# A chunked RWKV7 kernel: the state turned by VectorE transposes, state and score products joined into one of 128 rows, 40 columns for w

## The chip, the cores and the metric

The kernel runs on one core of a Trainium2 chip. The metric is the device time of one execution in microseconds (us). Most executions of one kernel lie within a per cent or so; a run more than 1.5% above the fastest of its kernel is called slow and is left out of the ratios. TensorE does the matmuls, VectorE (DVE in the profile) the elementwise work, ScalarE (ACT) copies and activations, GpSimd (POOL) three multiplications per unit, and the sync queue (SP) issues most transfers. The **granted clock** is the TensorE clock that the profile shows, as a share of full speed. An **eviction** is the copy of a matmul's result out of its PSUM bank, where the matmuls write, by VectorE or ScalarE.

## The reference

For each of 4 batches and 8 heads, a 40x40 state runs through 768 tokens. A feed-forward block with SiLU follows. All of it is float32.

```python
def _attn_ref(r, k, v, w, a, b):              # each (4, 8, 768, 40)
    state = np.zeros((B, H, D, D))
    for t in range(S):
        y[:, :, t] = einsum('bhd,bhde->bhe', r_t, state)
        Sa = einsum('bhde,bhe->bhd', state, a_t)
        state = state * w_t[:, :, None, :] - einsum('bhd,bhe->bhde', Sa, b_t)
        state = state + einsum('bhd,bhe->bhde', v_t, k_t)

def _moe_ref(x, w_in, w_out):                 # x: 3072 x 320, d_ff = 2048
    h = x @ w_in
    return ((h / (1.0 + np.exp(-h))) @ w_out).astype(np.float32)
```

## The kernel before

The 768 tokens are cut into 12 chunks of 64. Batches go in two pairs, so a chunk has two **units** and there are 24 units. A unit passes through `keys` (transposes), `right` (right-hand sides), `solve`, `read`, `write` (new state and outputs) and `turn` (the state transposed for the next chunk's `write`). Two chunks ahead, `prepare` scales the inputs (VectorE scan and reciprocal, then GpSimd) and makes the negated scores. Once per two chunks, `invert` inverts the triangular matrices of both: the scores go out to memory and back, then 31 rows are worked off one after another on VectorE, then merged. That falls in the **odd** chunks. The feed-forward block, called **moe** here, is woven in between as soon as two chunks of outputs are there. The order of each engine's instructions is fixed when the kernel is built. The line numbers (L501 and so on) are those of the profile.

```python
# prepare, two chunks ahead
def scale():
    ...                                                                   # VectorE scan, L262
    pin(nc.vector.reciprocal(R, u.W[:, :, 1 : C + 1]))                    # L263, 3.35 us
    nc.gpsimd.tensor_tensor(out=u.a, in0=u.a, in1=u.W[:, :, 0:C], op=ALU.mult)               # L264
    nc.gpsimd.tensor_tensor(out=u.kb[:, :, 1], in0=u.kb[:, :, 1], in1=R, op=ALU.mult)        # L265
    ...                                                                   # the third multiplication, L271
...
def between(u, n, s):      # scores: n=1 negated, for the inverse; n=0 for the scores times v
    pm = [bank("pm") for _ in range(2)]
    ...
    nc.tensor.matmul(pm[j][C * be : C * be + C, p * C : p * C + C],       # L236, four 64x64 tiles
                     lhsT=u.kb[J, q, n, :], rhs=u.a[J, q, :], start=True, stop=True)
    ...                                                                   # masked evictions, L244
...
def row(t):                # the inverse: 31 rows, each needs the one before
    x = nc.vector.tensor_tensor(out=part, in0=X[L, :, t + 1 : N, t + 1 : N], in1=..., op=ALU.mult)     # L327
    x = nc.vector.tensor_reduce(out=X[L, :, t + 1 : N, t], in_=part, axis=AX.X, op=ALU.add)            # L334
...
# the unit's own chain
def right():
    between(u, 0, u.sk)
    pr = [bank("pr") for _ in range(2)]
    for p in range(P if u.n > 0 else 0):
        for be in range(2):
            nc.tensor.matmul(pr[be][C * be : C * be + C, p * 80 : p * 80 + 80],              # L513
                             lhsT=u.a[:, P * be + p, :], rhs=gbd[:, P * be + p], start=p == 0, stop=False, ...)
    for p in range(P):
        for j in range(2):
            for be in range(2):
                mark["right"] = nc.tensor.matmul(pr[be][R, p * 80 + j * D : p * 80 + j * D + D],   # L525
                             lhsT=u.sk[R, j, p, :], rhs=u.v2[R, 2 * p + j, :], ...)
...
def turn():
    pt = [bank("pt") for _ in range(2)]
    for q in range(Q):
        for j in range(2):
            mark["turn"] = nc.tensor.matmul(pt[j][DP * j : DP * j + D, q * DP : q * DP + DP],      # L587
                             lhsT=gbd[J, q, j], rhs=ident[J, J], start=True, stop=True).ins
    for j in range(2):
        nc.scalar.copy(out=gt[R].rearrange("p q e -> p (q e)"), in_=pt[j][R])                     # L596
```

Of the kernel before, what the change touches and what calls it, by code (L numbers as in the profile page):

```python
# [27 lines left out]
DP = 64  # L28
# [13 lines left out]
def kernel(  # L42
# [37 lines left out]
    ms = sb.tile([128, 2, C], F32, name="ms")  # L80
# [3 lines left out]
    nc.vector.tensor_copy(out=ms[:, 0], in_=ml)  # L84
    nc.vector.tensor_scalar(out=ms[:, 1], in0=ml, scalar1=-1.0, scalar2=None, op0=ALU.mult)
# [8 lines left out]
    Gbd = [sb.tile([128, Q, 2, D], F32, name=f"Gbd{m}") for m in range(NM)]  # L94
    GT = [sb.tile([128, Q, DP], F32, name=f"GT{m}") for m in range(NM)]
    RHS = [sb.tile([128, P, 2, DP], F32, name=f"RHS{m}") for m in range(NM)]
# [111 lines left out]
    def load(u, what="abk", queue=nc.sync):  # L208
        B2 = slice(2 * u.m, 2 * u.m + 2)
        if "a" in what:  # L210
            u.a = sb.tile([128, Q, C], F32, name="a", bufs=4)
            send(queue, u.a.rearrange("p (b q) t -> p b (q t)", b=2), aT[B2, u.n].rearrange("b p c -> p b c"))
        if "b" in what:
            u.kb = sb.tile([128, Q, 2, C], F32, name="kb", bufs=6)
        for n, x in ((1, bT), (0, kT)):
            for be in range(2 if "kb"[n] in what else 0):
                send(queue, u.kb[:, P * be : P * be + P, n], x[2 * u.m + be, u.n].rearrange("p (q t) -> p q t", q=P))
# [10 lines left out]
    def between(u, n, s):  # L228

        pm = [bank("pm") for _ in range(2)]  # L230
        for p in range(P):
            for be in range(2):
                for j in range(2):
                    q = P * be + p
                    J = slice(DP * j, DP * j + DP)
                    nc.tensor.matmul(  # L236
                        pm[j][C * be : C * be + C, p * C : p * C + C],
                        lhsT=u.kb[J, q, n, :],
                        rhs=u.a[J, q, :],
                        start=True,  # L240
                        stop=True,
                    )
        for j in range(2):
            x = nc.vector.tensor_tensor(  # L244
                out=s[:, j],
                in0=pm[j][:, 0 : P * C].rearrange("p (q t) -> p q t", q=P),
                in1=ms[:, n].unsqueeze(1).to_broadcast([128, P, C]),
                op=ALU.mult,
            )
            if n == 1 and u.n < 2:  # L250
                in_order(x, "vector")

    sbs, mark = {}, {}

    def pre(u, md):
        def scale():
            u.W = sb.tile([128, Q, C + 1], F32, name="W", bufs=6)
            R = u.w[:, :, 1 : C + 1]
            pin = partial(in_order, line="vector") if u.n < 2 else lambda x: x
            for be in range(2):  # L260
                W, w = (x[:, P * be : P * be + P].rearrange("p q t -> p (q t)") for x in (u.W, u.w))
                pin(nc.vector.tensor_tensor_scan(W, w, one.rearrange("p q t -> p (q t)"), 0.0, ALU.mult, ALU.add))  # L262
            pin(nc.vector.reciprocal(R, u.W[:, :, 1 : C + 1]))  # L263
            nc.gpsimd.tensor_tensor(out=u.a, in0=u.a, in1=u.W[:, :, 0:C], op=ALU.mult)  # L264
            nc.gpsimd.tensor_tensor(out=u.kb[:, :, 1], in0=u.kb[:, :, 1], in1=R, op=ALU.mult)  # L265
            if u.n > 1:
                keys()
# [9 lines left out]
        def scores():  # L277
            if u.m == 0:
                sbs[u.n] = sb.tile([128, NM, 2, P, C], F32, name="sb", bufs=2)
            between(u, 1, sbs[u.n][:, u.m])  # L280
# [180 lines left out]
    def load_v(u):  # L461
        u.v2 = sb.tile([128, H, D], F32, name="v2", bufs=2)
        T = slice(C * u.n, C * u.n + C)
        for be in range(2):
            nc.sync.dma_start(u.v2[C * be : C * be + C].rearrange("p h d -> p (h d)"), v[2 * u.m + be, T, :])

    def load_r(u, wait=None):
        u.r = sb.tile([128, Q, C], F32, name="r", bufs=2)
        u.vut = sb.tile([128, Q, 2, C], F32, name="vut", bufs=2)
# [20 lines left out]
    def chain(u, xs):  # L490
        X = XT[u.n % 2][:, u.m]
        gbd, gt, rhs = Gbd[u.m], GT[u.m], RHS[u.m]
# [13 lines left out]
        def right():  # L506
            u.sk = sb.tile([128, 2, P, C], F32, name="sk", bufs=2)
            between(u, 0, u.sk)
            pr = [bank("pr") for _ in range(2)]

            for p in range(P if u.n > 0 else 0):
                for be in range(2):
                    nc.tensor.matmul(  # L513
                        pr[be][C * be : C * be + C, p * 80 : p * 80 + 80],
                        lhsT=u.a[:, P * be + p, :],
                        rhs=gbd[:, P * be + p],
                        start=p == 0,
                        stop=False,
                        skip_group_check=True,
                    )  # L520
            for p in range(P):
                for j in range(2):
                    for be in range(2):
                        R = slice(C * be, C * be + C)
                        mark["right"] = nc.tensor.matmul(  # L525
                            pr[be][R, p * 80 + j * D : p * 80 + j * D + D],
                            lhsT=u.sk[R, j, p, :],
                            rhs=u.v2[R, 2 * p + j, :],
                            start=u.n == 0 and p == 0 and j == 0,
                            stop=True,  # L530
                            skip_group_check=True,
                        )
            for be in range(2):
                R = slice(C * be, C * be + C)
                x = nc.scalar.copy(
                    out=rhs[R, :, :, 0:D],
                    in_=pr[be][R, 0 : H * D].rearrange("p (q j d) -> p q j d", q=P, j=2),
                )
                if u.n == 0:
                    behind(x, issued["scalar"])  # L540

        def solve():
            pu = [bank("pu") for _ in range(2)]
            pw = [bank("pw") for _ in range(2)]
# [3 lines that stand above are left out]
# [4 lines left out]
                            rhs=rhs[R, p, j, 0:D],  # L552
# [10 lines left out]
            for p in range(P):  # L563
                for j in range(2):
                    for be in range(2):
                        R = slice(C * be, C * be + C)
                        nc.tensor.matmul(
                            pw[be][DP * j : DP * j + DP, p * C : p * C + C],
                            lhsT=rhs[R, p, j, :],
                            rhs=X[R, P * j + p, :],  # L570
                            start=True,
                            stop=True,
                        )
            for be in range(2):
                nc.scalar.activation(
                    out=u.vut[:, P * be : P * be + P, 1, :],
                    in_=pw[be][:, 0 : P * C].rearrange("p (q t) -> p q t", q=P),
                    func=AF.Copy,
                    scale=-1.0,
                )  # L580

        def turn():
            pt = [bank("pt") for _ in range(2)]
            for q in range(Q):
                for j in range(2):
# [3 lines left out]
                        lhsT=gbd[J, q, j],  # L589
# [28 lines left out]
        def write():  # L618
# [25 lines left out]
            for be in range(0 if last else 2):  # L644
                for j in range(2):
                    J = slice(DP * j, DP * j + DP)
                    g = gbd[J, P * be : P * be + P, j]
                    nc.vector.tensor_tensor(out=g, in0=gy[be][J, :, 0:D], in1=g, op=ALU.add)  # L648
            for j in range(0 if last else 2):
                J = slice(DP * j, DP * j + DP)  # L650
                g = gbd[J, :, j]
# [127 lines left out]
    for t in RHS + Gbd + GT + XT:  # L779
# [242 lines left out]
```

## Time and profile before

| | before |
|---|---|
| time, median of 3 runs | 963.82 us (963.7 to 967.04) |
| span of the profiled run | 967.4 us |
| TensorE / VectorE busy | 86% / 58% |
| chunks 4 to 9, pairs of an even and an odd one | 132.5, 129.5, 123.0 us |

The page and the windows are shown in the prediction. One view also belongs here: VectorE's timeline where odd chunk 7 begins (its key transposes start at 560.06 us). Columns of a timeline: start us, duration us, engine, line, operation, output and inputs, shapes, number of instructions in the step, and in brackets the idle time ahead with what ended it.

```profile
558.41 1.28 DVE L262 TENSOR_TENSOR_SCAN W<-w,one 128x260 f32<-128x260 f32 x2
...
559.92 3.34 DVE L263 RECIPROCAL w<-W 128x512 f32<-128x512 f32 x1
...
574.25 3.35 DVE L263 RECIPROCAL w<-W 128x512 f32<-128x512 f32 x1
...
592.27 0.15 DVE L327 TENSOR_TENSOR tmp<-XI,mi 128x1 f32<-128x1 f32 x1
```

The first unit's scan and reciprocal run as the odd chunk opens, the second unit's 14 us later, and the first row of the inverse 32.2 us after the keys. This is a chain: scan, reciprocal, GpSimd, scores, eviction, the scores' way through memory, rows. VectorE's busy share does not show it.

### The profile page before, as it was taken

To read this page: it belongs to the slowest core of one execution; us is meant where nothing else is said; L and a number is where in the kernel's file an instruction comes from. 1 tells how busy PE (TensorE), PEld (TensorE's weight loads), DVE (VectorE), ACT (ScalarE), POOL (GpSimd) and SP (SyncE) were. 2 spreads that over 40 slices of the span, in tenths; PEclk is the share of its full clock that TensorE was granted. 3 is DMA by queue.
4 is the path that set the end of the run, shared out by engine and by line. 5 is a ranking of instruction groups with operands and counts; after the bars stand their busy time and mean duration, and the time that the engine had idled before them with its cause. 6 is when DMAs were issued, how large, how long until landed. Compare 5 with 4: busy or idle time off the path is not lost.

```text
span 967.4 us, 26530 instructions
## 1 busy us (share of the span) xinstructions
PE 833.7 (86%) x11586; PEld 588.1 (61%) x11586; DVE 564.6 (58%) x1141; ACT 290.9 (30%) x661; POOL 97.4 (10%) x98
## 2 busy tenths in 40 slices
PE   2247088979999949999989999899999999999996
PEld 2236077745778814787646876548865577755544
DVE  8777988976216798164894366972649823031120
ACT  3144356531323212332213341224231142210110
POOL 5121021100001110001010020200110000000000
PEclk9999558989759979997999999999999999999999
DMA  6975516542115530445512555223522213002001
GB/s 141 206 182 128 139 49 171 143 107 65 44 41 137 116 94 18 97 106 113 137 38 45 124 120 119 69 55 92 117 58 62 83 35 73 2 8 66 1 0 31
DMA packets 217626, 83.06 MB, mean 86 GB/s; under 512 B 181536, under 2 KB 209440, under 8 KB 217504
## 3 DMA queue, kind: packets, MB, share of 16 engines
q1 hardware_dynamic: 202384, 76.98, 33.7%
q10 hardware_dynamic: 15120, 4.33, 2.3%
q8 instruction: 92, 1.51, 0.6%
q14 instruction: 30, 0.25, 0.1%
HBM read 67.11 MB, written 14.16 MB: 84 GB/s over the span
## 4 chain that ended last, share of the span: by engine, by line
PE 58%; DVE 28%; DMA 6%; issue 3%; ACT 2%; SPq 1%; POOL 0%; ACTq 0%; POOLq 0%; DVEq 0%
PE po L714 16%; PE ph L698 11%; DVE tmp L327 5%; DVE XI L334 4%; PE pl L603 4%; PE ph L703 4%; DVE w L263 3%; PE pm L236 3%; PE pt L501 3%; PE pq L429 2%; PE pu L549 2%; PE pr L525 2%; DVE gts L707 2%; DVE Gbd L648 2%; PE po L446 2%
## 5 line engine op out<-in xcount | busy, mean ns | idle before, releaser
L714 PE MATMUL po<-wo_s,gts 128*128 128x320 f32 x768 | 221.6, 441 | 5.2 <-DVE gts L707 5.2
L698 PE MATMUL ph<-xt,wi_s 128*128 128x512 f32 (+1 forms) x448 | 195.9, 575 | 25.4 <-DVE gts L707 14.9
L714 PEld LDWEIGHTS po<-wo_s,gts 128*128 128x128 f32 x768 | 142.1, 190 | 67.1 <-DVE gts L707 7.2
L698 PEld LDWEIGHTS ph<-xt,wi_s 128*128 128x128 f32 x448 | 83.9, 201 | 110.9 <-issue 58.2
L707 DVE TENSOR_TENSOR gts<-ph,sg 128x512 f32<-128x512 f32 (+1 forms) x112 | 65.6, 607 | 137.7 <-ACT sg L706 137.6
L706 ACT ACTIVATE sg<-ph 128x512 f32<-128x512 f32 (+1 forms) x112 | 54.4, 533 | 234.8 <-PE ph L703 234.6
L327 DVE TENSOR_TENSOR tmp<-XI,mi 64x2 f32<-64x2 f32 (+40 forms) x169 | 80.8, 478 | 14.4 <-DMA mi<-md 10.8
L263 DVE RECIPROCAL w<-W 128x512 f32<-128x512 f32 x24 | 80.3, 3347 | 1.1
L334 DVE TENSOR_REDUCE XI<-tmp 64x2 f32<-64x2 f32 (+40 forms) x169 | 76.2, 451 | 3.9
L236 PE MATMUL pm<-a,kb 64*64 64x64 f32 x1536 | 48.9, 240 | 18.4 <-POOL kb L265 17.4
L703 PE MATMUL ph<-xt,wl_s 64*128 64x512 f32 (+1 forms) x224 | 62.2, 602 | 0.0
L265 POOL TENSOR_TENSOR kb<-kb,w 128x512 f32<-128x512 f32 x24 | 29.3, 1219 | 302.4 <-DVE w L263 232.4
L244 DVE TENSOR_TENSOR sk<-pm,ms 128x256 f32<-128x256 f32 x48 | 18.1, 416 | 68.8 <-PE pm L236 68.7
L236 PEld LDWEIGHTS pm<-a,kb 64*64 64x64 f32 x1536 | 39.5, 148 | 30.2 <-POOL kb L265 19.7
L264 POOL TENSOR_TENSOR a<-a,W 128x512 f32<-128x512 f32 x24 | 28.6, 1190 | 269.1 <-DMA a<-in_aT 175.2
L603 PEld LDWEIGHTS pl<-r,vut 64*128 64x128 f32 x768 | 49.9, 205 | 6.6 <-issue 2.8
L603 PE MATMUL pl<-r,vut 64*128 64x64 f32 x768 | 51.0, 290 | 2.7 <-DVE vl L611 2.6
L611 DVE TENSOR_TENSOR vl<-pl,ml 128x512 f32<-128x512 f32 x48 | 31.2, 684 | 35.9 <-PE pl L603 35.6
L596 ACT COPY GT<-pt 40x512 f32<-40x512 f32 x44 | 25.5, 580 | 80.9 <-PE pt L587 80.4
L525 PE MATMUL pr<-v,sk 64*64 64x40 f32 x768 | 34.5, 234 | 16.8 <-ACT kt L502 15.6
L525 PEld LDWEIGHTS pr<-v,sk 64*64 64x64 f32 x768 | 29.9, 141 | 22.7 <-ACT kt L502 15.7
L380 PE MATMUL pq<-XT,sb 16*32 16x16 f32 x512 | 8.9, 195 | 39.3 <-DVE XT L371 32.5
(90 smaller groups left out, 1065.2 us busy)
## 6 DMA issues: line engine op xcount, KB each, us to landing
vut<-in_vT SPq DMA_DIRECT2D x48, 128.0 KB
r<-in_rT SPq DMA_DIRECT2D x24, 256.0 KB
a<-in_aT SPq DMA_DIRECT2D x22, 256.0 KB
kb<-in_bT SPq DMA_DIRECT2D x44, 128.0 KB
kb<-in_kT SPq DMA_DIRECT2D x44, 128.0 KB
w<-in_wT SPq DMA_DIRECT2D x41, 128.0 KB
room<-in_w_out SPq DMA_DIRECT2D x20, 256.0 KB
room<-in_w_in SPq DMA_DIRECT2D x16, 256.0 KB
```

The costliest lines, as they stand in the source:

```text
L236: nc.tensor.matmul(pm[j][C * be : C * be + C, p * C : p * C + C], lhsT=u.kb[J, q, n, :], rhs=u.a[J, q, :], start=True, stop=True,)
L263: pin(nc.vector.reciprocal(R, u.W[:, :, 1 : C + 1]))
L327: x = nc.vector.tensor_tensor(out=part, in0=X[L, :, t + 1 : N, t + 1 : N], in1=M[L, :, t, t + 1 : N].unsqueeze(2).to_broadcast([hi - lo, I ...
L334: x = nc.vector.tensor_reduce(out=X[L, :, t + 1 : N, t], in_=part, axis=AX.X, op=ALU.add)
L525: mark["right"] = nc.tensor.matmul(pr[be][R, p * 80 + j * D : p * 80 + j * D + D], lhsT=u.sk[R, j, p, :], rhs=u.v2[R, 2 * p + j, :], start ...
L603: nc.tensor.matmul(pl[j][:, q * C : q * C + C], lhsT=u.vut[J, q].rearrange("p n t -> p (n t)"), rhs=u.r[J, q, :], start=True, stop=True,)
L611: nc.vector.tensor_tensor(out=u.vl[:, :, j, D:], in0=pl[j].rearrange("p (q t) -> p q t", q=Q), in1=ml.unsqueeze(1).to_broadcast([128, Q, C ...
L698: in_order(nc.tensor.matmul(ph[n], lhsT=wi_s[:, k, at : at + 128], rhs=xt[:, k, :], start=k == 0, stop=False))
L703: in_order(nc.tensor.matmul(ph[n], lhsT=wl_s[R, i, :], rhs=xt[R, 2, :], start=False, stop=True))
L706: nc.scalar.activation(out=sg, in_=ph[n], func=AF.Sigmoid)
L707: nc.vector.tensor_tensor(out=place(2 * i + n), in0=ph[n], in1=sg, op=ALU.mult)
L714: in_order(nc.tensor.matmul(po[:, 0:DM], lhsT=place(f)[:, b * 128 : b * 128 + 128], rhs=wo_s[:, NF // 2 * half + f, :], start=f == 0, stop ...
```

## The change

Its intent is to take work from the busiest engine, TensorE. The turn's 32 matmuls with the identity become eight VectorE transposes of 32-row blocks, from chunk 2 on. State and v go into one tile (GV), and scaled a and the scores k·a into another, so that two products become one of 128 rows. w is computed with 40 columns instead of 64. In exchange a comes in two transfers and v in four, GpSimd scales a in two halves, and the score evictions are of 64x512 instead of 128x256.

```diff
-    Gbd = [sb.tile([128, Q, 2, D], F32, name=f"Gbd{m}") for m in range(NM)]
+    GVf = [sb.tile([128, 2 * Q * D + 32], F32, name=f"GV{m}") for m in range(NM)]
+    GV = [x[:, 0 : 2 * Q * D].rearrange("p (j q d) -> p j q d", j=2, q=Q) for x in GVf]
...
-            nc.gpsimd.tensor_tensor(out=u.a, in0=u.a, in1=u.W[:, :, 0:C], op=ALU.mult)
+            for j in range(2):
+                J = slice(DP * j, DP * j + DP)
+                nc.gpsimd.tensor_tensor(out=u.a[J, j], in0=u.a[J, j], in1=u.W[J, :, 0:C], op=ALU.mult)
...
+    def keyed(u):
+        pm = bank("pm")
+        for q in range(Q):
+            for j in range(2):
+                J = slice(DP * j, DP * j + DP)
+                O = slice(DP - DP * j, 2 * DP - DP * j)
+                nc.tensor.matmul(
+                    pm[O, q * C : q * C + C], lhsT=u.kb[J, q, 0, :], rhs=u.a[J, j, q, :], start=True, stop=True
+                )
+        for j in range(2):
+            O = slice(DP - DP * j, 2 * DP - DP * j)
+            nc.vector.tensor_tensor(out=u.a[O, j], in0=pm[O]..., in1=ml[O]..., op=ALU.mult)
...
         def right():
-            between(u, 0, u.sk)                # and the two groups of matmuls above
+            keyed(u)
+            pr = bank("pr")
+            ...
+                        mark["right"] = nc.tensor.matmul(
+                            pr[C * be : C * be + C, h * D : h * D + D],
+                            lhsT=u.a[:, j, P * be + p, :],
+                            rhs=gv[:, j, P * be + p, :],
+                            start=True, stop=True,
+                        )
...
-                            pw[be][DP * j : DP * j + DP, p * C : p * C + C],
+                            pw[be][DP * j : DP * j + D, p * C : p * C + C],
...
         def turn():
+            if u.n > 1:
+                wide = GVf[u.m]
+                for j in range(2):
+                    for e in range(2):
+                        for d in range(2):
+                            E, T = (slice(DP * j + 32 * x, DP * j + 32 * x + 32) for x in (e, d))
+                            at = j * Q * D + 32 * d
+                            nc.vector.transpose(
+                                out=gt[T, :, 32 * e : 32 * e + 32],
+                                in_=wide[E, at : at + Q * D].rearrange("p (q d) -> p q d", q=Q)[:, :, 0:32],
+                            )
+                return
```

## The prediction

> **What bounds the kernel now.** I read the page first: busy shares, slices, chain of waits.
>
> ```profile
> PE 833.7 (86%) x11586; PEld 588.1 (61%) x11586; DVE 564.6 (58%) x1141; ACT 290.9 (30%) x661; POOL 97.4 (10%) x98
> PE   2247088979999949999989999899999999999996
> DVE  8777988976216798164894366972649823031120
> PE 58%; DVE 28%; DMA 6%; issue 3%; ACT 2%; SPq 1%; POOL 0%; ACTq 0%; POOLq 0%; DVEq 0%
> ```
>
> A slice is 24.2 us. In the first eight (190 us) VectorE is at 7 to 9 tenths and TensorE mostly low: VectorE bounds the start. From there TensorE is at 9 nearly everywhere, and VectorE's peaks recur once per pair of chunks. Since a busy TensorE need not be a limiting one, I then took the table of windows, cut where the chunks' key transposes (L501) begin:
>
> ```profile
> 301.80:398.40 96.60, 82.00 (x917) 53.97 (x915) 68.63 (x120) 25.40 (x57) 12.10 (x10) 0.93 0.35 84
> 530.90:560.10 29.20, 28.23 (x760) 25.05 (x759) 12.42 (x30) 11.63 (x25) 2.36 (x2) 1.00 0.52 122
> 560.10:660.40 100.30, 96.12 (x953) 58.70 (x953) 71.80 (x126) 27.27 (x60) 12.53 (x10) 0.98 0.37 85
> ```
>
> The columns are length, then busy us of TensorE, its weight loads, VectorE, ScalarE, GpSimd, the clock, the DMA share, GB/s. The second line is chunk 6, the third chunk 7: 129.5 us per pair, TensorE idle for 29.20 - 28.23 + 100.30 - 96.12 = 5.2 us of it. Chunk 3 (first line) is the exception: 14.6 us idle, of which the waits name 9.3 us for one moe input and 4.8 us for VectorE. After 868 us only moe products are left. So from chunk 4 on each us of TensorE's order that disappears should nearly be a us of the end.
>
> How long a group holds TensorE is not its busy time (matmuls overlap) but start to start, from the timeline:
>
> ```profile
> 400.25 0.69 PE L236 MATMUL pm<-a,kb 64*64 64x64 f32 x32
> 400.87 1.12 PE L513 MATMUL pr<-Gbd,a 128*64 128x80 f32 x16
> ...
> 405.10 1.01 PE L525 MATMUL pr<-v,sk 64*64 64x40 f32 x28
> 406.04 0.88 PE L429 MATMUL pq<-XT,sb 32*32 32x32 f32 x42
> ...
> 606.75 1.09 PE L587 MATMUL pt<-ident,Gbd 64*40 64x64 f32 x32
> 607.77 3.50 PE L714 MATMUL po<-wo_s,gts 128*128 128x320 f32 x12
> ```
>
> Every f32 product is two matmuls. Per unit (half a chunk, 24 in all) the scores hold TensorE 0.62 us, the state's product 1.06, the scores' product 28 matmuls in 0.94, so 1.07 for 32; the turn of the state 1.02.
>
> **What the Trainium skill says.** "TensorE: Matmul & The Clock Gate", Part 3, says that weight loads overlap running matmuls only in other row groups, and that tiles of the array run side by side. The trace agrees in kind: 64x64 scores, spread over four tiles, take 0.62/32 = 19 ns each, the turn, on two diagonal tiles, 1.02/32 = 32 ns. "TensorEngine Tiling (Array Packing)", Key Properties, says that a change of tiling mode drains the engine; the trace has steps such as 0.62 us for work whose starts span 0.48, which fits. The same page says that row tiles should not use one PSUM bank at once; the new scores do that. But L380 already has four row groups in one bank and ran 122 matmuls in 1.13 us, 9 ns each, so I expect no penalty. "VectorE: DVE Perf Modes", The three transpose paths, calls the VectorE transpose fastest within 32x32 blocks. The only ones in this trace (L371, 32x512) take 0.70 us, and the full state needs four blocks of them per half, so here the point is not speed but which engine pays.
>
> **The change part by part.**
>
> 1. *Turn.* Units of chunks 2 to 10 (18) lose 32 matmuls each: 1.02 us x 18 = 18.4 us of TensorE. ScalarE loses two copies (580 ns). VectorE gains 8 transposes of 32x256. Fixed part and slope: 128x256 against 128x512 from PSUM are 0.415 and 0.681 us, 1.04 ns an element; the 0.702 us transpose then has a fixed 0.17, and 256 elements take about 0.44 us (estimate). 8 x 0.44 = 3.5 us a unit, 63 us in all.
>
> 2. *One product.* Before: 0.62 + 1.06 + 1.07 = 2.75 us. After: the scores go to two diagonal tiles, since state channels in rows j must meet scores in rows 1-j. L625 (64x64, 64 columns, two diagonal tiles) starts 32 matmuls in 0.93 us, so 1.0 for them; 0.38 us more than now. Then 32 matmuls of 128 rows by 40 columns; L513 does 16 of 80 columns with starts spanning 0.54 us, 36 ns each, so 30 ns at 40 columns, about 1.0 us. With a change of mode, 2.2 us: 0.55 us less, x 24 = 13 us, 10 of them in chunks 2 to 10. On VectorE the two evictions become 64x512 (L611 has this length in 0.681) instead of 128x256 (0.415): +0.53 us x 24 = 13 us. ScalarE saves one of two copies of 0.42.
>
> 3. *40 columns for w.* 32 matmuls at L567 take 0.66 us by starts; weight loads of 40 instead of 64 columns may save 0.1 us, 2 us in all. ScalarE pays four short activations for two of 0.381 us: +0.76 a unit.
>
> 4. *Moves.* v comes in pieces of 160 bytes, in 4 transfers a unit instead of 2, into the tile that holds the state, so next chunk's v must wait for this chunk's product. The last of the eight blocks of a transpose also reaches into the v columns, so it probably waits for the turn too. GpSimd scales a in two halves of about 1.19 us each instead of one. "DMA: Bandwidth & Descriptors", Specifications, puts the smallest line-rate transfer at 512 bytes; here 181536 of 217626 packets are already below it and the queue's share is 33.7%, so bandwidth is not short.
>
> Sum of TensorE: 18.4 + 13 + 2 = 33 us at most. Chunks 0 and 1 sit in the start that VectorE and transfers set: minus 2. Chunk 3 is partly held by VectorE, so its 3 us are mostly lost. That leaves about 28 us.
>
> **The rivals.**
>
> *VectorE takes it back.* It gains 63 + 13 = 76 us, to 641 us, 66% of the present span. On average there is room: chunk 6 goes from 12.4 to about 20.5 of 29 us, chunk 7 from 72 to 80 of 100. But an in-order engine with 3.5 us of transposes delays what stands behind:
>
> ```profile
> 603.49 3.34 DVE L263 RECIPROCAL w<-W 128x512 f32<-128x512 f32 x1
> 606.75 0.27 DVE L334 TENSOR_REDUCE XI<-tmp 128x13 f32<-128x169 f32 x1
> 606.94 0.30 DVE L648 TENSOR_TENSOR Gbd<-pgy,Gbd 64x160 f32<-64x160 f32 x1
> ...
> 613.62 0.68 DVE L707 TENSOR_TENSOR gts<-ph,sg 128x512 f32<-128x512 f32 x1
> ...
> 614.35 0.81 PE L714 MATMUL po<-wo_s,gts 128*128 128x320 f32 x2 [3.08 <-DVE gts L707]
> ```
>
> Here the state updates, the inverse's rows and one 3.34 us reciprocal stood ahead of a moe eviction, and TensorE lost 3.08 us. The transposes join exactly there, in odd chunks. For it: this wait. Against it: such waits total only 2 to 4 us in each of chunks 5, 7 and 9, and the order is made anew with the added work known. I charge 1.5 to 2 us for each odd chunk 5, 7, 9 and 3 in chunk 3: 8 us. If VectorE became the bound in every odd chunk, it would cost some 6 us in each of four, 24 us, and the time would be about 958.
>
> *A new wait for v or the scores.* The product now needs both evictions (2 x 0.68 us) where the state's product used to cover the first; TensorE's order will be filled with moe products or the other unit's scores, as now (L714 between the halves of L525). From even to odd chunks the turn begins at 685.4 and the next L525 at 696.1; transposes end perhaps 5 us later than the turn did, transfers in the chain take 2.2 to 4.5 us, and the issuing queue takes 0.6 us for each. The second unit's v may be 1 us late in four such places: 4 us.
>
> *The transfers or GpSimd.* GpSimd is busy 10% and its extra 1.2 us lies beside the 3.35 us reciprocal that it waits for anyway. I give this nothing but a us or two at the start.
>
> *Row tiles in one bank do serialise.* Then the new scores cost 32 x about 60 ns = 2 us, 1 us more, 24 us in all, and the time would be about 965. L380's 9 ns speaks against it.
>
> **Range and chances.** 28 us less 8 for VectorE and 2 for v and the start leaves 18 to 19 us: 963.8 - 18.8 = 945. Nearly all realised gives 930; VectorE bound in odd chunks, with late v, gives 961. The 2% line is 944.5, so the chances of faster and same are even: 0.48 and 0.48, with 0.04 for slower.
>
> **What would show it.** The turn's matmuls gone but for chunks 0 and 1; 144 transposes near 0.44 us; the new scores' starts near 30 ns, not 60; the product of 128 rows near 1 us; right() near 2.2 us a unit. The pair of chunks 6 and 7 should shrink from 129.5 to about 125 us, more in the even chunk than in the odd. Waits of L714 and L698 for gts growing beyond 4 us in an odd chunk would show the first rival, waits of the product for v the second. I am wrong if scores serialise, if transposes take 0.7 us as the longer ones do, or if the new order of instructions brings stalls or gains that have nothing to do with these sums.

## The result

The kernel after took 1004.27 us (median of 4 runs, 995.21 to 1013.75), the kernel before beside it 963.76 us (959.79 to 967.04). The ratio is 1.0391, with a 95% interval of 1.0298 to 1.0483: **slower by 3.9%**. Here and below a ratio is the mean time of one kernel's fast runs over that of the other's fast runs of the same rounds, so it is not quite the ratio of the medians. The profiled run of after spans 993.0 us. It was the fastest of its four, so the two traces account for 25.6 us of the 38 us.

First the page of after: the busy line, then the slices of TensorE, of VectorE and of TensorE's clock (a slice is 24.8 us).

```profile
PE 814.7 (82%) x10658; PEld 563.1 (57%) x10658; DVE 645.0 (65%) x1284; ACT 280.8 (28%) x649; POOL 126.5 (13%) x124
...
PE   2149089989996639998979989889999699989997
...
DVE  8776998976337699348798376897295992541211
...
PEclk9555568999897769999999998899998799999999
```

TensorE has 19 us less busy time in a span that is 25.6 us longer. Its row now has a hole in the thirteenth to fifteenth slice (6, 6, 3), which lie in chunk 3, and a 6 in the thirty-second, in chunk 9; VectorE is at 7, 6, 9 and at 9 there. The table of windows, cut at the key transposes as before, with chunk 3, chunk 6 and chunk 7:

```profile
298.80:415.30 116.50, 80.07 (x801) 52.47 (x799) 88.16 (x157) 22.69 (x51) 14.07 (x12) 0.81 0.33 74
...
556.50:583.90 27.40, 27.06 (x666) 22.65 (x664) 10.87 (x22) 11.40 (x25) 4.71 (x4) 1.00 0.48 112
583.90:700.30 116.40, 105.07 (x883) 62.74 (x876) 92.15 (x166) 25.79 (x57) 14.40 (x12) 0.93 0.36 77
```

Chunk 6 shrank from 29.2 to 27.4 us, chunk 7 grew from 100.3 to 116.4. All chunks from 2 on, from the same two traces:

| stretch, us | before | after | change |
|---|---|---|---|
| odd chunks 3, 5, 7, 9 | 96.6, 102.6, 100.3, 93.5 | 116.5, 113.3, 116.4, 107.5 | +60.7 |
| even chunks 2, 4, 6, 8, 10 | 46.7, 29.9, 29.2, 29.5, 35.7 | 36.5, 27.9, 27.4, 27.5, 26.0 | -25.7 |
| chunk 11 to the end | 148.3 | 131.7 | -16.6 |
| start to chunk 2 | 255.1 | 262.3 | +7.2 |

The sum is +25.6 us. The odd chunks took the time and more; part of it came back at the end, because moe products that used to be left for the end (240 matmuls of L714 after the start of chunk 11) had been done in the longer odd chunks (192 of L744 left). Chunk 7 of after ran all 128 second-layer moe matmuls that a pair has, where before it ran 104. The time in which TensorE runs neither a matmul nor a weight load, from chunk 2 on, went from 31.5 to 79.0 us. In chunks 3 and 9 the longest piece of it (17.7 and 9.0 us) was spent waiting for the next piece of moe's input. Chunk 7 idled at its start and in the middle, 4.2 us behind one VectorE result at 641.6 us, but was busy again from 685 to 700 us.

VectorE's timeline of after where odd chunk 7 begins (keys at 583.94), to be held against the one shown of before:

```profile
585.98 3.15 DVE L608 STREAM_TRANSPOSE GT<-GV 32x256 f32<-32x256 f32 x7
...
590.50 3.59 DVE L608 STREAM_TRANSPOSE GT<-GV 32x256 f32<-32x256 f32 x8
594.13 1.41 DVE L273 TENSOR_TENSOR a<-pm,ml 64x512 f32<-64x512 f32 x2
595.46 1.27 DVE L289 TENSOR_TENSOR_SCAN W<-w,one 128x260 f32<-128x260 f32 x2
...
597.24 3.33 DVE L290 RECIPROCAL w<-W 128x512 f32<-128x512 f32 x1
...
610.91 3.35 DVE L290 RECIPROCAL w<-W 128x512 f32<-128x512 f32 x1
...
629.92 0.16 DVE L356 TENSOR_TENSOR tmp<-XI,mi 128x1 f32<-128x1 f32 x1
630.11 0.43 DVE L608 STREAM_TRANSPOSE GT<-GV 32x256 f32<-32x256 f32 x1
630.58 0.15 DVE L363 TENSOR_REDUCE XI<-tmp 128x1 f32<-128x1 f32 x1
```

The even chunk's turn, 16 transposes of two units, stands ahead of the odd chunk's first scan. The first reciprocal comes 13.3 us after the keys (it was at -0.1), the second 27.0 us after (14.2), and the first row 46.0 us after (32.2). So 13.8 of the odd chunk's 16.1 us are there before the first row. Not all of that is the transposes: they take 7.2 us, and the changed kernel without any turn (n2, below) already has its first row at 40.6 us. Then the odd chunk's own turns begin among the rows, a transpose between every two row instructions: the rows' 56.9 us hold 6.5 us of transposes (in before the rows took 53.6 us). VectorE was busy for 93 to 97% of the rows' time in the odd chunks of before, after and n1.

The waits of TensorE between 262 and 993 us of after (total us, times, longest):

```profile
PE ph L728 <- DMA xt<-xs: 26.6, 2, 17.7
PE ph L728 <- DVE gts L737: 13.8, 8, 5.3
PE pr L545 <- DVE a L273: 7.5, 8, 2.2
PE ph L728 <- DVE ot L756: 6.7, 3, 4.2
PE pm L244 <- POOL a L293: 6.1, 4, 4.1
...
PE pm L244 <- POOL kb L294: 5.6, 3, 4.0
```

and in before, from 255 us on:

```profile
PE ph L698 <- DMA xt<-xs: 9.3, 1, 9.3
PE ph L698 <- DVE gts L707: 7.7, 4, 4.6
PE po L714 <- DVE gts L707: 5.2, 4, 3.1
```

Of the 47.5 us that were added, the moe input (xt) is 17.3, the wait for GpSimd's scaled inputs (a and kb) 9.4, and the eviction of moe's output (ot) 6.3. The moe evictions (gts) hardly grew, from 12.9 to 13.8. In chunk 3 the store of the last piece of moe's input was issued at 349.1 us, in before at 341.0. The wait for L273 is new: the joined product waits 7.5 us for the evictions of its scores. Finally the groups that answer to the sums of the prediction (busy us, mean ns):

```profile
L293 POOL TENSOR_TENSOR a<-a,W 64x512 f32<-64x512 f32 x48 | 57.2, 1192 | 258.4 <-DMA a<-in_aT 126.4
...
L608 DVE STREAM_TRANSPOSE GT<-GV 32x256 f32<-32x256 f32 x144 | 62.6, 435 | 3.0
...
L273 DVE TENSOR_TENSOR a<-pm,ml 64x512 f32<-64x512 f32 x48 | 33.1, 689 | 44.3 <-PE pm L268 43.1
```

The transposes (435 ns against an estimate of 0.44 us), the evictions (689 ns against 0.68 us) and the GpSimd halves were all as predicted. The durations are not what failed.

### The profile page after: what moved, and what is told of

The parts are those of the page before. It is cut to its first block, busy times and chain, and to the rows that moved or that the text cites. A ratio compares the mean times of both kernels' runs of the same rounds, so it can differ in the third digit from the quotient of the medians.

```text
span 993.0 us, 25013 instructions
## 1 busy us (share of the span) xinstructions
PE 814.7 (82%) x10658; PEld 563.1 (57%) x10658; DVE 645.0 (65%) x1284; ACT 280.8 (28%) x649; POOL 126.5 (13%) x124
## 3 DMA queue, kind: packets, MB, share of 16 engines
q1 hardware_dynamic: 225008, 76.98, 33.8%
## 4 chain that ended last, share of the span: by engine, by line
PE 39%; DVE 17%; issue 8%; POOL 1%; DMA 1%; ACT 1%; SPq 0%; DVEq 0%; POOLq 0%
PE po L744 13%; PE ph L728 9%; DVE GT L608 3%; DVE tmp L356 3%; PE ph L733 3%; DVE w L290 3%; PE pl L633 3%; DVE XI L363 3%; PE pr L545 2%; PE pu L565 1%; PE pm L268 1%; PE pq L458 1%; PE pgy L665 1%; DVE gts L737 1%; PE po L475 1%
## 5 line engine op out<-in xcount | busy, mean ns | idle before, releaser
L728 PE MATMUL ph<-xt,wi_s 128*128 128x512 f32 (+1 forms) x448 | 206.7, 593 | 53.4 <-DMA xt<-xs 26.6
L744 PE MATMUL po<-wo_s,gts 128*128 128x320 f32 x768 | 217.3, 440 | 1.1 <-DVE wo_s L175 1.1
L744 PEld LDWEIGHTS po<-wo_s,gts 128*128 128x128 f32 x768 | 144.5, 191 | 66.6 <-issue 4.3
L728 PEld LDWEIGHTS ph<-xt,wi_s 128*128 128x128 f32 x448 | 84.3, 205 | 141.1 <-issue 56.9
L293 POOL TENSOR_TENSOR a<-a,W 64x512 f32<-64x512 f32 x48 | 57.2, 1192 | 258.4 <-DMA a<-in_aT 126.4
L608 DVE STREAM_TRANSPOSE GT<-GV 32x256 f32<-32x256 f32 x144 | 62.6, 435 | 3.0
L273 DVE TENSOR_TENSOR a<-pm,ml 64x512 f32<-64x512 f32 x48 | 33.1, 689 | 44.3 <-PE pm L268 43.1
L641 DVE TENSOR_TENSOR vl<-pl,ml 128x512 f32<-128x512 f32 x48 | 31.1, 685 | 45.4 <-PE pl L633 45.3
L303 ACT ACTIVATE junk<-w 128x512 bf16<-128x512 f32 x24 | 15.1, 629 | 133.5 <-DVE w L290 82.2
L545 PE MATMUL pr<-GV,a 128*64 128x40 f32 x768 | 34.3, 244 | 18.7 <-DVE a L273 8.7
L545 PEld LDWEIGHTS pr<-GV,a 128*64 128x64 f32 x768 | 29.3, 151 | 34.4 <-issue 13.2
L268 PE MATMUL pm<-a,kb 64*64 64x64 f32 x768 | 32.1, 235 | 19.8 <-ACT kt L534 17.9
L244 PE MATMUL pm<-a,kb 64*64 64x64 f32 x768 | 25.0, 250 | 27.9 <-POOL kb L294 21.1
```

The lines of the kernel that those rows point to most:

```text
L293: nc.gpsimd.tensor_tensor(out=u.a[J, j], in0=u.a[J, j], in1=u.W[J, :, 0:C], op=ALU.mult)
L545: mark["right"] = nc.tensor.matmul(pr[C * be : C * be + C, h * D : h * D + D], lhsT=u.a[:, j, P * be + p, :], rhs=gv[:, j, P * be + p, :], ...
L608: nc.vector.transpose(out=gt[T, :, 32 * e : 32 * e + 32], in_=wide[E, at : at + Q * D].rearrange("p (q d) -> p q d", q=Q)[:, :, 0:32],)
L728: in_order(nc.tensor.matmul(ph[n], lhsT=wi_s[:, k, at : at + 128], rhs=xt[:, k, :], start=k == 0, stop=False))
L744: in_order(nc.tensor.matmul(po[:, 0:DM], lhsT=place(f)[:, b * 128 : b * 128 + 128], rhs=wo_s[:, NF // 2 * half + f, :], start=f == 0, stop ...
```

## The experiments

Sixteen kernels ran, in four groups, each group on one chip beside the kernel before (its median was 960.18, 963.01, 967.19 and 964.15 us). The main theories were these. **VectorE**: the transposes delay the chain of the odd chunks. **The product**: joining the two products costs, for itself, more than it saves. **The queue** (Q): the loads of v, which in after write into the tile that the turn reads, stand behind the transposes in the sync queue and hold up all that follows. **w** (W): four loads of a instead of two ahead of the next w in that queue delay the second unit's scan. The theory at the outset was VectorE. For the runs that move the transposes, the texts before the runs name two forms of it: **C**, the chain alone is what costs, and **L**, the 63 us of VectorE's load cost time wherever they stand.

### Which part of the change costs what

**e1_pe_turn**: after, with the turn on TensorE in every chunk, so the joined product and the 40 columns alone.

```diff
         def turn():
-            if u.n > 1:
-                ...                    # the eight transposes
-                return
             pt = [bank("pt") for _ in range(2)]
```

> The changed kernel with the turn back on TensorE in all chunks; product of 128 rows and 40 columns stay. Theory T (the transposes fill VectorE in the odd chunks and hold up the moe input, the moe evictions and the scores' evictions): 945 to 965 us, so at or under the kernel before, idle time of TensorE from chunk 2 on back from 79 to about 40 us. Theory P (the product's own new waits: evictions of 64x512 with nothing to cover them, v in the state's tile, the scaling of a in two halves on GpSimd): 985 to 1005 us, waits of the product and for GpSimd as in the changed kernel.

Measured: 971.77 us, ratio to before 1.0113 [1.0049, 1.0177]. The joined product is no gain at all but costs about 1%. The time lies between the ranges of the two theories and fits neither.

**e2_turn_only**: before, with the VectorE turn from chunk 2 on and nothing else. (Two small edits only made room for the padded state tile.)

```diff
-    Gbd = [sb.tile([128, Q, 2, D], F32, name=f"Gbd{m}") for m in range(NM)]
+    Gf = [sb.tile([128, 2 * Q * D + 24], F32, name=f"Gbd{m}") for m in range(NM)]
+    Gbd = [x[:, 0 : 2 * Q * D].rearrange("p (q j d) -> p q j d", j=2, q=Q) for x in Gf]
...
         def turn():
+            if u.n > 1:
+                ...                    # eight nc.vector.transpose, as in after
+                return
```

> The kernel before with the turn by VectorE from chunk 2 on and nothing else (a pad of 24 columns behind the state, four small tiles merged to make room). Theory T: 980 to 1005 us. Theory P: 945 to 965 us, since 18 us of TensorE go and VectorE has room on average.

Measured: 982.47 us, ratio 1.0236 [1.0149, 1.0323]. The turn alone is a loss too, as the theory VectorE had it. Its runs had a granted clock of 0.929 to 0.934 and in one case 0.891; before had 0.936 to 0.941 in six of seven. That difference is too small to be the cause: two runs of n1 (below) took 951.96 and 951.98 us at 0.898 and 0.934.

**n1_no_turn** and **n2_no_turn_changed**: before and after with no turn at all from chunk 2 on. Their results are wrong; the work that remains is the same. They separate what TensorE gains from what VectorE pays.

```diff
         def turn():
+            if u.n > 1:
+                return
```

> Wrong result on purpose: the kernel before with no turn at all from chunk 2 on (the turned state stays zero), so 18 us of TensorE and 36 copies of ScalarE go and nothing comes in. The prediction's theory (each us of TensorE from chunk 4 on is a us of the end): 940 to 946 us. Theory C: the odd chunks stay at 93 to 103 us, as VectorE's chain is not shortened, and the gain is 12 us or less: 948 to 962 us.

> Wrong result on purpose: the changed kernel with no turn at all from chunk 2 on. Beside the changed kernel (1.039) it gives what the 144 transposes cost. Theory C: 0.99 to 1.01 of the kernel before, so 30 to 45 us for 63 us of transposes; and against the kernel before with no turn (0.988) what the product and the 40 columns cost without any turn: 0 to 2%. If the product's part is the main loss: 1.02 to 1.03.

Measured: n1 951.97 us, ratio 0.9879 [0.9795, 0.9963]; n2 972.05 us, ratio 1.0048 [0.9983, 1.0112]. n1 fell in the range that its text gives for the chain, n2 likewise. n1, which adds nothing to VectorE, already has the wait of moe for VectorE that was to show the first rival. Of the waits of TensorE from 262 to 960 us, first a line of n1:

```profile
PE ph L700 <- DVE gts L709: 14.8, 6, 5.3
```

and the same wait in e2, with the transposes:

```profile
PE ph L713 <- DVE gts L722: 18.8, 7, 5.6
```

So this wait hardly tells the two apart; TensorE's idle time does. From chunk 2 on it was 36.4 us in n1 and 64.2 in e2, 52.6 in n2 and 79.0 in after. The four kernels and e1 give a table:

| step | from two ratios | in us (1% = 9.64) | TensorE idle, us |
|---|---|---|---|
| turn taken off TensorE, put nowhere | n1 / before: -1.2% | -12 | +4.9 |
| 144 transposes put on VectorE | e2 / n1: +3.6% | +35 | +27.8 |
| the same, in the changed kernel | after / n2: +3.4% | +33 | +26.4 |
| joined product, 40 columns | e1 / before: +1.1% | +11 | +14.8 |
| the same, without turns | n2 / n1: +1.7% | +16 | +16.2 |

Minus 12, plus 33 to 35, plus 11 to 16 makes 32 to 39 us; the whole change measured 38 us by its ratio. The steps by way of n1 and n2 add up by construction; the test is that e2 (+2.4%) and e1 (+1.1%), each alone, make 3.5% against 3.9%. The ratios come from different groups, each with an interval of about 0.6 to 0.9% to either side, so a step is known to some 6 to 12 us.

### Where the transposes cost

**e4_even_only**: after, with the VectorE turn in even chunks only; odd chunks turn on TensorE.

```diff
-            if u.n > 1:
+            if u.n > 1 and u.n % 2 == 0:
```

> The changed kernel with VectorE's turn in even chunks alone (VectorE is busy 12 of 29 us there); odd chunks turn on TensorE. Theory T: the loss of the odd chunks goes, 950 to 970 us. Theory P: 980 to 1005 us.

Measured: 995.23 us, ratio 1.0366 [1.0312, 1.042]. Against e1 of the same group, 80 of the 144 transposes cost 2.5%, 24 us net of what they spare TensorE. After, in another group, is only 0.3% above e4. So the transposes of the even chunks, which fall at the start of the odd chunk's chain, seem to carry most of the loss. Its text had expected 950 to 970 us if the transposes were the cause; that missed, since e1 itself was slow, and the time lies in the range given for the product.

**d1_later** (of after) and **d2_later_turn_only** (the same on e2): each VectorE turn is moved into the next chunk, behind its solve; the odd chunks' turns also behind the last row of the inverse.

```diff
-                            nc.vector.transpose(
+                            x = nc.vector.transpose(
...
+                            if u.n % 2 == 1:
+                                behind(x, mark["row"])
...
-        return [keys, right, solve, read, write] + ([] if last else [turn])
+        u.turn = turn
+        return [keys, right, solve, read, write] + ([turn] if u.n < 2 else [])
...
+        if n > 2:
+            steps[6:6] = [u.turn for u in units[n - 1]]
```

> The changed kernel with each VectorE turn moved in the program into the next chunk, behind its solve, and those of odd chunks kept behind the last row of the inverse; the same 144 transposes. Theory C (an odd chunk is as long as a chain on VectorE: scan, reciprocal, scores, inverse; the transposes stood ahead of its start and inside its rows): the first scan of an odd chunk starts near 0.3 us after the keys again, not 13.6, rows take about 50 us instead of 56, odd chunks about 100 us; 950 to 970 us in all. Theory L (the 63 us of VectorE's load cost wherever they stand): 990 to 1010 us.

> The kernel before with the VectorE turn alone, moved as in the run of the changed kernel with the later turn. Theory C: 945 to 965 us, at least 15 us under the same kernel with the turn at its old place (982). Theory L: 975 to 990 us.

Measured: d1 1005.04 us, ratio 1.0417 [1.0331, 1.0503]; d2 977.99 us, ratio 1.0141 [1.0069, 1.0214]. In d1's chunk 7 the first scan is back, 1.5 us before the keys, but the transposes then stand from 7 or 8 to 17 or 20 us and hold up the second unit's scan: the first row still comes at 42 to 46 us. In d1 the delay had moved, not gone; in d2 the first row came at 38 to 40 us (e2 42 to 51) and the time was 0.95% under e2's. Both times lie in the ranges that were given for L. (The scan times in the text for d1, 0.3 and 13.6 us, are some 2 us late: the traces of before and after have -1.7 and 11.5.)

**d3_gap_turn_only** (of e2) and **d4_gap** (of after): as d1 and d2, but the even turns wait for the second unit's score evictions, so that they fall into the gap while the scores travel through memory.

```diff
+                            behind(x, mark["row" if u.n % 2 == 1 else "sb"])
```

> The kernel before with the VectorE turn alone; those of even chunks are kept behind the second eviction of negated scores in the next chunk (the place where VectorE waits for the round trip of the scores through memory), those of odd chunks behind the last row of the inverse. Theory C: neither scan nor reciprocal nor rows wait for a transpose any more, the first row comes 33 to 38 us after the keys, and the time nears that of the kernel with no turn at all (952): 952 to 966 us. Theory L (the load itself costs): 972 to 985 us.

> The changed kernel with the transposes in the same gap. If the transposes' place were all of its loss, 950 to 965 us; if the product's part keeps the 11 us that it lost with the turn on TensorE (972), 965 to 985 us; if place does not matter, 995 to 1010 us.

Measured: d3 979.2 us, ratio 1.0123 [1.0053, 1.0193]; d4 995.47 us, ratio 1.0283 [1.0226, 1.034]. VectorE's timeline of d3 in a like odd chunk:

```profile
593.24 3.35 DVE L267 RECIPROCAL w<-W 128x512 f32<-128x512 f32 x1
597.91 0.69 DVE L726 TENSOR_TENSOR gts<-ph,sg 128x512 f32<-128x512 f32 x1 [1.32 <-ACT sg L725]
...
600.28 7.20 DVE L595 STREAM_TRANSPOSE GT<-Gbd 32x256 f32<-32x256 f32 x16
607.51 2.48 DVE L629 TENSOR_TENSOR vl<-pl,ml 128x512 f32<-128x512 f32 x4
```

The 16 transposes now run as one block of 7.2 us in the gap, and the first row is back at 34.5 to 38.1 us after the keys (n1 34.5 to 41.4). The time fell by 1.1% in each pair (e2 to d3, after to d4). Each of the two has an interval of its own of about 1.1% to either side, so it is likely by both together rather than certain. TensorE's idle time fell from 64.2 to 47.8 us and from 79.0 to 57.4. So the position probably explains about a third of the 3.4 to 3.6%. The traces show why it is no more (sums in us, chunk starts as in the windows):

| | before | n1 | e2 | d3 | n2 | after | d4 |
|---|---|---|---|---|---|---|---|
| odd chunks 3 to 9: keys to first row | 142 | 153 | 180 | 147 | 171 | 185 | 160 |
| first to last row | 194 | 188 | 215 | 199 | 188 | 213 | 194 |
| last row to the next keys | 57 | 56 | 54 | 65 | 58 | 56 | 66 |
| even chunks 2 to 10 | 171 | 146 | 146 | 160 | 149 | 145 | 167 |

The transposes (n1 to e2) lengthen the way to the first row by 27 us and the rows by 26, and the gap takes most of both back: the odd chunks of d3 are 38 us shorter than those of e2, those of d4 34 us shorter than those of after. But of this some 26 and 30 us return in the even chunks and after the start of chunk 11. So the chain sets the length of an odd chunk, but it does not set the total alone. All four runs of d1 to d4 fell in the ranges given for L, none in those for C. Yet d3 is still 2.5% above n1 (1.0123 / 0.9879): 144 transposes cost some 24 us even where they do not delay the first row. TensorE also was busy for 825.6 us in d3's profile against 810.7 in n1's with the same 11010 matmuls (d4 836.8 against n2 819.9). A part may be the clock: in chunk 2, before d3's first transpose, TensorE is already busy 45.4 us against 39.5 at a clock of 0.66 against 0.71. The rest stays unexplained.

**f4_gap_even**: before with the even turns alone on VectorE, in the gap, and the odd ones on TensorE (the edit is shown against d3).

```diff
-            if u.n > 1:
+            if u.n > 1 and u.n % 2 == 0:
...
-        if n > 2:
+        if n > 2 and n % 2 == 1:
             steps[6:6] = [u.turn for u in units[n - 1]]
```

> The kernel before with VectorE's turn for the even chunks only, kept behind the second eviction of negated scores in the odd chunk; odd chunks turn on TensorE. It takes 4 chunks' turn, 8 us, from TensorE and puts 28 to 35 us on VectorE into a place where it waits for memory. Theory C: 0.99 to 1.005. If even there the load costs: 1.01 to 1.02.

Measured: 979.3 us, ratio 1.0142 [1.0094, 1.0189]. Even in the best place that was found, and with only 80 transposes, there is a loss, as L expected (1.01 to 1.02). So the delay of the first row is not all of the cause; what the rest waits for stays open. The loss is not far above what a neutral reordering cost (f2 below, 0.8%).

**e3_v_apart**: after, with a pad behind each half of GV so that no transpose reads a column of v (small tiles were merged to make room). It tests Q.

```diff
-    GVf = [sb.tile([128, 2 * Q * D + 32], F32, name=f"GV{m}") for m in range(NM)]
+    GVf = [sb.tile([128, 2 * (Q * D + 32)], F32, name=f"GV{m}") for m in range(NM)]
...
-                            at = j * Q * D + 32 * d
+                            at = j * (Q * D + 32) + 32 * d
```

> The changed kernel with 32 columns of pad behind each half of the state's tile, so that no transpose reads a column of v and the load of v waits for the product alone. Theory Q (the loads of v stand in the sync queue until the transposes are done and hold the moe input and later loads behind them): 965 to 985 us, the moe input issued within 1 us of the last store of its rows, no wait of 17 us. Theory T: 990 to 1010 us, as the changed kernel.

Measured: 1020.83 us (1008.57 to 1027.26). Its two fast runs average 1012.9 us, 5.4% above the mean of the seven runs of before beside it. In chunk 3 of its trace moe's input is fetched 2.8 us after the last store was issued, in after 5.0: the coupling was gone. That did not help, so Q is not the cause. The time got worse, by 1 to 2% against after, though no work was added; the likeliest reason, only argued, is that the order made at build time changed.

### Why the joined product does not gain

Each side cost of the joined product was put into the kernel before by itself.

**e5_w_40**: 40 columns for w, with the turned values in two fixed tiles.

```diff
-                            pw[be][DP * j : DP * j + DP, p * C : p * C + C],
+                            pw[be][DP * j : DP * j + D, p * C : p * C + C],
...
+                for j in range(2):
+                    R = slice(DP * j, DP * j + D)
+                    nc.scalar.activation(out=u.vut[R, P * be : P * be + P, 1, :], ...)
```

> The kernel before with 40 columns for w alone (two fixed tiles for the turned values, four activations of 40 partitions instead of two of 128 a unit). Predicted worth 2 us on TensorE: 957 to 967 us. If the extra ScalarE work (0.76 us a unit) holds up the moe sigmoids: 966 to 975 us.

**e6_scale_in_halves**: GpSimd scales a in two halves of 64 rows.

```diff
-            nc.gpsimd.tensor_tensor(out=u.a, in0=u.a, in1=u.W[:, :, 0:C], op=ALU.mult)
+            for j in range(2):
+                J = slice(DP * j, DP * j + DP)
+                nc.gpsimd.tensor_tensor(out=u.a[J], in0=u.a[J], in1=u.W[J, :, 0:C], op=ALU.mult)
```

> The kernel before with GpSimd's scaling of a in two halves of 64 rows, nothing else. If this step of the new layout costs by itself (1.2 us on the way to each pair of scores, and so into VectorE's chain once or twice per odd chunk): 966 to 978 us. If it lies beside the reciprocal, as predicted: 958 to 965 us.

**e7_small_loads**: a in two transfers, v in four of 160-byte pieces.

```diff
+            for j in range(2):
+                J = slice(DP * j, DP * j + DP)
+                send(queue, u.a[J]..., aT[B2, u.n, J]...)
...
+        for j in range(2):
+            for be in range(2):
+                nc.sync.dma_start(u.v2[...]..., v[2 * u.m + be, T, :].rearrange("s (p j d) -> j s p d", j=2, d=D)[j])
```

> The kernel before with the loads of the changed one alone: a in two transfers of 64 rows, v in four of 160-byte pieces, into the old tiles. If the sync queue's issue time (three more issues of 0.6 us a unit, ahead of w and of the moe input) is what the product's part loses: 968 to 978 us, and VectorE waiting for w in chunk 3. If not: 958 to 966 us.

Measured: e5 967.33 us, ratio 1.0038 [0.997, 1.0106]; e6 966.58 us, 1.0032 [0.9956, 1.0108]; e7 973.54 us, 1.0057 [0.9996, 1.0118]. None can be told from zero, and none is a gain. e7's time lies in the range that its text gives for an effect of the queue, but its ratio is not clear of 1. Together they would make the 1.1%, but that sum is an argument, not a measurement.

**f1_w_first** (of e1) and **f2_w_first_before** (of before): the second unit's load of a is issued behind the next w instead of ahead of it. They test W, which came from e1's chunk 3. From e1's timelines of VectorE and of TensorE there:

```profile
326.60 1.29 DVE L289 TENSOR_TENSOR_SCAN W<-w,one 128x260 f32<-128x260 f32 x2 [3.25 <-DMA w<-in_wT]
```

```profile
332.74 1.23 PE L244 MATMUL pm<-a,kb 64*64 64x64 f32 x32 [8.50 <-POOL kb L294]
```

The scan waited for w (the queue issued it 11.9 us after the keys, in before 7.2), and TensorE then waited 8.5 us for GpSimd behind it.

```diff
                 load_w(units[k // NM][k % NM], w0)
+                if u.m == 0 and u.n > 3:
+                    load(units[u.n][1], "a")
...
-            load(u)
+            load(u, "abk" if u.m == 0 else "bk")
```

> The changed kernel with the turn on TensorE (972, 1.1% over the kernel before), and the second unit's load of a issued after the next load of w. Theory W (w waits in the sync queue behind loads of a, whose buffer the new product releases later, and holds the second scan): the second scan of an odd chunk comes 2 to 4 us earlier, the 8.5 us wait for GpSimd in chunk 3 goes, 0.99 to 1.003 of the kernel before. If the wait moves to a itself: 1.008 to 1.02.

> Control: the kernel before with the same order of loads. Theory W: w was hardly held there (the second scan 13 to 15 us after the keys), so 0.99 to 1.005. If it gains as much as the run with the new product does, the order of loads is a gain of its own and not what the product lost.

Measured: f1 984.55 us, ratio 1.0178 [1.0124, 1.0233]; f2 974.15 us, 1.0082 [1.0034, 1.0129]. The local effect was there: in f1 the second scan of chunk 3 came 12.2 us after the keys instead of 16.4, and no wait for GpSimd was above 4.8 us. The time was no better, so W is not borne out. f2, expected at 0.99 to 1.005, shows a harmless-looking reordering costing 0.8%. So the 1.1% of e1 and of the gap, single pairs of kernels each, cannot be surely told from what any remade order may do; the 3.4 to 3.6% of the transposes can.

No kernel with a right result beat the kernel before.

## Why the prediction was wrong

Predicted: 945 us, 930 to 961. Measured: 1004. By its own terms:

| term of the sum, us | predicted | measured |
|---|---|---|
| turn off TensorE | -18 | -12 (interval -4 to -20) |
| VectorE takes back | +8 (rival: +24) | +33 to +35 |
| joined product and 40 columns | -15 | +11 to +16 |
| start, chunk 3, late v | +7 | within the above |

**The turn on TensorE was not wrong.** The profiles of n1 and before differ by 17.2 us, the ratios by 12, and the interval holds 18.

**The step that failed first is the term for VectorE**: "I charge 1.5 to 2 us for each odd chunk 5, 7, 9 and 3 in chunk 3: 8 us." The rival named the right mechanism but was also too small. Behind it lies the sentence "So from chunk 4 on each us of TensorE's order that disappears should nearly be a us of the end." It took TensorE's 96% in chunk 7 as the limit of chunk 7. The runs show another reading: n1 took 32 matmuls per unit away, and its odd chunks still lasted 91.8 to 103.6 us (before 93.5 to 102.6). An odd chunk is as long as its chain to the last row plus 13 to 16 us in nearly every one of them (up to 20 in d1 to d4), and moe products fill TensorE beside it. The transposes lengthened that chain both ahead of the first row and among the rows, by about equal parts (27 and 26 us in four odd chunks of e2). In after, TensorE then idled more for the most part behind the moe input, GpSimd's results and the eviction of moe's output. The prediction looked at waits of moe evictions (3 us) for the size of the effect; those waits hardly grew (12.9 to 13.8 us), and in n1 they are nearly as large as in e2. Its hope that "the order is made anew with the added work known" did not come true either: the transposes were placed where they became possible.

The gap placement recovers 1.1 of the 3.4 to 3.6%. So the delay of the chain's start is likely a part. The rest, some 2.4%, was paid in every place that was tried, as L has it; by what way isn't explained.

**The second failed step is the joined product**: "With a change of mode, 2.2 us: 0.55 us less, x 24 = 13 us". Start to start, the step to the next group included, the new scores and the new product took 37 to 39 ns a matmul where 30 was expected, so `right` holds TensorE for 2.4 us in e1 and in after (from chunk 4 on) against 2.6 in before: 0.1 to 0.2 us a unit, at most 5 us in 24 units. The 2.75 of the prediction rests on one unit whose state product took 1.06; it takes 0.81 on average over chunks 4 to 11. Row tiles that share a bank did not serialise: two-tile groups over two banks (L587, L625) take 35 to 36 ns in before. Nor did TensorE's busy time fall with the joined product (before 833.7 us, e1 833.0). And about 15 us of TensorE idle time came with it, in three pairs of kernels alike, mostly in chunk 3 in e1. Some of the cost also stands ahead of chunk 2, which begins at 262 to 267 us in every kernel with the joined product and at 253 to 260 in those without it; the one exception among these is e7 (262.5), so the small loads may be the cause. (With the joined product 32 more moe matmuls are done by then, so not all of this is lost.) Which of the side costs makes it is open: e5, e6 and e7 give 0.3 to 0.6% each, and f1 removed one wait without effect.

**What held**: 144 transposes of 435 ns; evictions of 689 ns; bandwidth was not short (the queue's share was 33.7% and is 33.8%); the even chunk did shrink (29.2 to 27.4 us), and the prediction's own mark, the pair of chunks 6 and 7 at about 125 us, showed at once where it failed: 143.8.

The lower clock in the slow places looks like a companion rather than a cause. The Trainium skill, "TensorE: Matmul & The Clock Gate", Part 1, says that throttling is the default state and activity releases it. The traces agree in part: 0.81 in chunk 3 of after, where TensorE idles for 36 us, and 1.00 in chunk 6, where it idles for 0.3; but chunk 2 of before has 0.72 with only 2.7 us idle.

## What to carry to other kernels

Before moving work to an engine that has room on average, follow the chain that sets the length of each stage and ask what will stand behind the new work in it; a filler such as moe makes the filled engine look like the limit. The best place for the new work is not free either: here it still cost some 24 of 35 us. Measure the two halves of such a trade apart, by a kernel that leaves the work out altogether (here -12 us) and one that only adds it on the other side (+35 us). Where a build-time order is remade by each edit, run neutral edits as controls: here a mere reordering of two loads moved the time by 0.8%, so differences of that size are not to be explained from one pair of kernels.

## What the Trainium skill lacked or had wrong

- "Perfetto Trace Analysis", Identifying the Most-Contended Engine, takes the engine of highest occupancy as the one to relieve first, TensorE being judged by its weight loads. Here TensorE (weight loads 61% busy, matmuls 86%) was relieved at the cost of VectorE (58%), and the time rose by 3.9%; the page lacks a warning that a filler can make up the occupancy.
- "TensorEngine Tiling (Array Packing)", Gotcha 1, says that different row tiles cannot access the same PSUM bank at once. The new scores write different partitions of one bank from two row tiles, gave right results, and took 37 to 39 ns a matmul, where groups of two tiles over two banks take 35 to 36; four row groups at L380 took 9 ns. So as a rule for a whole bank it is wider than what the runs show.
- "VectorE: DVE Perf Modes", The three transpose paths, has one time, for bf16. In float32 a transpose of 32x256 took 0.435 us here and one of 32x512 0.702.
- "GPSIMD Engine Reference" states that each of its cores has its own 16 partitions but gives no example of what that means for half a tile: multiplying 64x512 took 1.192 us, 128x512 1.190, so splitting by rows doubles the time.
